# Turning two more head pairs of batch 1 by crossbar DMA, and holding batch 2's loads back, in a fused attention and feed-forward kernel

## The chip, the cores and the metric

The kernel runs on one core of one Trainium2 chip. The metric is device time in microseconds (us) for one execution of the whole program. A profile's span is about 2 us shorter than the time of the same execution.

## The reference, cut to what matters

```python
# q, k, v: (batch 4, heads 8, seq 768, head_dim 64), float32
k_sum = k.reshape(B, H, 24, 32, D).max(axis=3)     # block maxima of the keys
v_sum = v.reshape(B, H, 24, 32, D).mean(axis=3)    # block means of the values
scores = softmax over [ local window of 31 keys | 24 blocks (+ log 32) ]
x = (scores @ [v, v_sum]) as (3072 tokens, 512)
g, val = x @ w_gate, x @ w_val                     # 512 x 1536 each
out = x + sigmoid(x @ w_res) * ((gelu(g) * val) @ w_out)
```

## The kernel before

The 3072 tokens are done in eight units of 384, two for each batch. In unit u TensorE runs twelve feed-forward steps (`fo` 0 to 11), each of four gate and four value products, then the output products of this unit, between which it puts the attention of unit u+1. Scores need keys and queries with head_dim on the partitions, so each pair of heads has to be transposed. For batches 2 and 3 the crossbar does this (DMA transposes issued from SP). For batch 1 TensorE does it in unit 1.

The names in the profiles: `tp` are transposes on TensorE, `g` and `vv` the gate and value products, `gvT` what VectorE makes of both (when it has, their buffers are free for TensorE again), `f` the output products, `s` the scores, `P` their exponentials, which VectorE multiplies by a mask, and `ao` the attention products. `vT` are the transposed values of a batch and `vsT` the block sums that VectorE takes of them. `kW` and `qT` are the transposed keys and queries, `km` and `ks` steps of the rest of the keys (`k_rest`). SPq and POOLq are the queues on which SP and GpSimd issue DMAs.

```python
def load_rows(b):                      # k, q (and v) rows of a batch, by head, issued from GpSimd
    for sb, src, name in (...)[0:2 if b == 1 else 3]:          # k, q, v in this order
        for h in range(H):
            nc.gpsimd.dma_start(out=sb[b][:, h // 2, :, h % 2 * D:...], in_=src[b, h]...)

def load_batch(b):
    load_rows(b)
    for c in range(NC + 1):            # seven value chunks in token order, into vext
        load_values(b, c)

def k_step(b, hp, pool, tag):          # six TensorE transposes, an ACT copy, then the rest
    tp = turn_pair(k_sb[b], hp, pool, tag)
    nc.scalar.copy(kw[:, :, OWN:OWN + QT]..., tp...)
    k_rest(kw)                         # VectorE: block maxima and neighbours, five instructions

def turn_batch(b, p0, p1):             # crossbar: two transposes for k, one for q, per pair
    for hp in range(p0, p1):
        for e in range(2):
            nc.sync.dma_start_transpose(out=kt[:, :, e, OWN:OWN + QT], in_=k_sb[b]...)
        nc.sync.dma_start_transpose(out=qT[b % 2][hp]..., in_=q_sb[b][:, hp]...)

def turn_values(b):                    # crossbar: four transposes, for the block means of v
    ...
# ---- in the loop over units, cut ----
if u == 1: load_batch(2)
for fo in range(FO):
    fo_step(st, gvT, fo)
    values_step(u, fo)     # VectorE: value copies; in units 2 and 4, steps 5 to 8, block_sums(vT)
    if u == 0 and fo == 4: load_batch(1)
    if u == 2 and fo == 8: gate(gvT[0:1, fo, 0:1]); load_rows(3)
    if half == 0 and 1 < nb < B and fo == 0:
        vT[nb] = turn_values(nb); turn_batch(nb, 0, NP - 1)
    if half == 1 and 1 < nb < B and fo == 0: turn_batch(nb, NP - 1, NP)
    if half == 1 and 1 < nb < B and 1 < fo < 2 + NP: k_rest(kW[nb % 2][fo - 2])
    if u == 1 and fo < 8:  # one pair per step: keys in steps 0 to 3, queries in 4 to 7
        ...k_step(nb, hp, *home) or q_step(q_sb[nb], nb, 0, S, hp, *home)
```

`gate` is a tiny GpSimd copy that reads a tile, so that GpSimd issues no later load before this tile is written. A batch's data live in `kW[b % 2]`, `qT[b % 2]` and `vext[b % 2]`.

The softmax here doesn't subtract the row's maximum and nothing guards it: scores larger than these inputs give would overflow.

## Time and profile before

| | |
|---|---|
| time, median of 3 runs | 265.78 us (265.74 to 267.43) |
| span of the profile | 263.4 us |
| TensorE busy | 254.6 us, 97% |
| VectorE, ScalarE busy | 174.0 us, 139.0 us |

GpSimd's timeline (start, length, engine, line, operation, output<-input, count, and in brackets the idle time before and what ended it): it shows when the loads of batch 2 are issued.

```profile
58.76 4.23 POOL L172 DMA_DIRECT2D k_sb<-in_k_dram  x5
64.19 0.83 POOL L172 DMA_DIRECT2D k_sb<-in_k_dram  x1 [1.21 <-DMA vext<-in_v_dram]
65.38 1.64 POOL L172 DMA_DIRECT2D k_sb<-in_k_dram  x2 [0.37 <-DMA vext<-in_v_dram]
67.01 6.75 POOL L172 DMA_DIRECT2D q_sb<-in_q_dram  x8
73.71 6.83 POOL L172 DMA_DIRECT2D v_sb<-in_v_dram  x8
80.48 5.79 POOL L99 DMA_DIRECT2D vext<-in_v_dram  x7
```

The last value chunk is issued at 86.3. The bracketed waits for an earlier DMA fit a program in which each load waits for the one issued eight before it to land. The second view is the tile vT, the transposed values, in the kernel before:

```profile
L233 SPq DMA_TRANSPOSE vT<-v_sb x8: 1213/1229/1288, 89.9 to 152.7; - x8
...
DMA to landing us min/median/max: 2.8/2.8/3.4
```

The four of batch 2 are issued from 89.9 on, 3 us after the last value chunk. They land in a median of 2.8 us (the first in 3.4), and VectorE takes the first block sum without a wait:

```profile
96.22 0.95 DVE L239 TENSOR_REDUCE vsT<-vT 128x24 bf16<-128x768 bf16 x1
```

### The profile page before, as it was taken

What the parts mean: (1) busy time and instruction counts of PE and PEld (TensorE: products, weight loads), DVE (VectorE), ACT (ScalarE), POOL (GpSimd) and SP (SyncE); (2) the same over time, 40 slices, a digit from 0 to 9 for tenths busy, and PEclk for the clock granted to TensorE, in tenths of its full rate; (3) what the DMA queues carried; (4) which work ended last, traced back from release to release, by engine and by line L of the source; (5) the groups of instructions that cost most, each with busy time, mean ns of one, the idle gap of its engine ahead of it and who ended that gap; (6) DMA issues with size and microseconds to landing.
All of it is one profiled execution on the core that took longest, in us unless ns stands there. A gap on an engine that the chain in (4) does not pass through costs nothing.

```text
span 263.4 us, 5865 instructions
## 1 busy us (share of the span) xinstructions
PE 254.6 (97%) x2324; PEld 143.9 (55%) x2324; DVE 174.0 (66%) x414; ACT 139.0 (53%) x240; POOL 93.5 (36%) x124
## 2 busy tenths in 40 slices
PE   6799999999999999999999999999999999999994
PEld 2546555566555555555545565556555665556543
DVE  3744863498476889877837899678738853574424
ACT  2845449657565536754365536653375537553310
POOL 7976533997999107998300000000000000000000
PEclk9999999999999999999999999999999999999999
DMA  5999999999999979999991466224001200020012
GB/s 82 171 172 197 197 206 189 147 177 176 118 117 127 201 126 110 158 173 181 144 48 44 115 119 103 46 82 100 2 1 42 80 0 2 36 86 1 2 40 80
DMA packets 109259, 27.64 MB, mean 105 GB/s; under 512 B 95408, under 2 KB 106288, under 8 KB 109232
## 3 DMA queue, kind: packets, MB, share of 16 engines
q0 software_dynamic: 86032, 16.26, 83.2%
q1 hardware_dynamic: 23200, 11.02, 18.0%
q8 instruction: 18, 0.29, 0.5%
q14 instruction: 9, 0.07, 0.1%
HBM read 32.51 MB, written 6.29 MB: 147 GB/s over the span
## 4 chain that ended last, share of the span: by engine, by line
PE 89%; POOL 3%; DMA 3%; DVE 2%; issue 1%; ACT 1%; POOLq 0%; DVEq 0%
PE f L394 24%; PE g L360 23%; PE vv L360 22%; PE r L378 8%; PE ao L328 4%; DMA vext<-in_v_dram 3%; PE s L296 2%; PE xp L347 2%; POOL vext L99 2%; PE tp L185 1%; PE vs L254 1%; DVE gvT L367 1%; PE gv L360 1%; PE wp L409 1%; POOL k L90 1%
## 5 line engine op out<-in xcount | busy, mean ns | idle before, releaser
L360 PE MATMUL g<-xT,w_gate 128*128 128x384 bf16 x380 | 77.8, 326 | 0.5 <-DVE gvT L367 0.5
L366 ACT ACTIVATE ge<-g 128x384 f32<-128x384 f32 x95 | 46.7, 492 | 59.5 <-PE g L360 30.3
L360 PE MATMUL vv<-xT,w_val 128*128 128x384 bf16 x380 | 77.8, 326 | 0.1
L367 DVE TENSOR_TENSOR gvT<-ge,vv 128x384 bf16<-128x384 f32 x95 | 51.9, 552 | 30.9 <-PE vv L360 27.6
L394 PE MATMUL f<-w_out,gvT 128*128 128x512 bf16 (+2 forms) x312 | 69.5, 363 | 0.0
L360 PEld LDWEIGHTS <-w_val 128*128 128x128 bf16 x384 | 37.5, 98 | 25.6 <-issue 1.0
L360 PEld LDWEIGHTS <-w_gate 128*128 128x128 bf16 x384 | 36.9, 98 | 25.1 <-issue 1.1
L394 PEld LDWEIGHTS <-gvT 128*128 128x128 bf16 x312 | 27.6, 98 | 25.6
L349 ACT COPY xT<-xp 128x384 bf16<-128x384 bf16 x32 | 15.1, 481 | 22.6 <-PE xp L347 22.6
L378 PE MATMUL r<-w_res,xT 128*128 128x512 bf16 x96 | 24.4, 380 | 0.0
L399 DVE SCALAR_TENSOR_TENSOR th<-th,f 128x512 f32<-128x512 f32 (+2 forms) x26 | 16.7, 642 | 11.4 <-PE f L394 8.5
L172 POOL DMA_DIRECT2D k_sb<-in_k_dram x24 | 20.1, 864 | 11.6 <-DMA w_out<-in_moe_w_out_dram 5.2
L99 POOL DMA_DIRECT2D vext<-in_v_dram x28 | 23.2, 866 | 0.9 <-PE g L360 0.6
L384 ACT ACTIVATE th<-r 128x512 f32<-128x512 f32 x24 | 14.2, 602 | 17.4 <-PE r L378 17.4
L313 DVE TENSOR_TENSOR P<-P,maskt 128x768 bf16<-128x768 bf16 x28 | 15.5, 557 | 10.3 <-ACT P L305 7.5
L172 POOL DMA_DIRECT2D q_sb<-in_q_dram x24 | 19.9, 862 | 0.0
L338 DVE TENSOR_TENSOR xn<-ao,rz 128x384 bf16<-128x384 f32 x32 | 17.8, 558 | 1.1
L305 ACT ACTIVATE P<-s,bias_t 128x768 bf16<-128x768 f32 x18 | 16.2, 903 | 3.1 <-PE s L296 2.9
L336 DVE RECIPROCAL rz<-ao 128x6 f32<-128x6 f32 x32 | 6.1, 190 | 17.4 <-PE ao L328 17.4
L401 DVE SCALAR_TENSOR_TENSOR o<-th,xn 128x512 f32<-128x512 f32 (+2 forms) x26 | 16.9, 651 | 0.9
L302 ACT ACTIVATE P<-s,bias_t 128x384 bf16<-128x384 f32 x28 | 14.6, 578 | 0.0
L172 POOL DMA_DIRECT2D v_sb<-in_v_dram x16 | 13.5, 874 | 1.2 <-DMA q_sb<-in_q_dram 0.7
(82 smaller groups left out, 218.4 us busy)
## 6 DMA issues: line engine op xcount, KB each, us to landing
out_dram<-o SPq DMA_DIRECT2D x23, 256.0 KB, 2.6
vext<-in_v_dram POOLq DMA_DIRECT2D x20, 128.0 KB, 6.6
k_sb<-in_k_dram POOLq DMA_DIRECT2D x24, 96.0 KB, 6.1
q_sb<-in_q_dram POOLq DMA_DIRECT2D x24, 96.0 KB, 4.4
w_gate<-in_moe_w_gate_dram POOLq DMA_DIRECT2D x6, 256.0 KB, 8.6
w_val<-in_moe_w_val_dram POOLq DMA_DIRECT2D x6, 256.0 KB, 8.8
w_out<-in_moe_w_out_dram POOLq DMA_DIRECT2D x3, 512.0 KB, 14.1
v_sb<-in_v_dram POOLq DMA_DIRECT2D x16, 96.0 KB, 5.0
```

The costliest lines, as they stand in the source:

```text
L99: nc.gpsimd.dma_start(out=dst, in_=v[b, :, lo:hi, :].rearrange("h p d -> p h d"))
L172: nc.gpsimd.dma_start(out=sb[b][:, h // 2, :, h % 2 * D:h % 2 * D + D], in_=src[b, h].rearrange("(c p) d -> p c d", c=NC))
L305: nc.scalar.activation(P.rearrange("p a t q -> p a (t q)"), s[:, :, 0:TU], AF.Exp, scale=scale, bias=bias_t[:])
L313: nc.vector.tensor_mul(Pf, Pf, maskt.unsqueeze(1).to_broadcast([128, 2 * HT, QT]))
L338: nc.vector.tensor_mul(xn, ao[:, :, :, 0:D], rz.to_broadcast([128, NSUB, 2, D]))
L360: nc.tensor.matmul(acc[:, 0:TU], w[:, ko, fs], st["xT"][:, ko, :], start=(ko == 0), stop=(ko == KO - 1))
L366: nc.scalar.activation(ge[:], g[:, 0:TU], AF.Gelu)
L367: nc.vector.tensor_mul(gvT[:, fo, :], ge[:], vv[:, 0:TU])
L378: nc.tensor.matmul(r[:], st["xT"][:, ko, ss], w_res[:, ko, :], start=(ko == 0), stop=(ko == KO - 1))
L394: nc.tensor.matmul(st["f", sub][:, 0:c1 - c0], gvT[:, fo, ss], w_out[:, fo, c0:c1], start=(fo == 0), stop=(fo == FO - 1))
L399: nc.vector.scalar_tensor_tensor(th, th, 1.0, f[:, 0:c1 - c0], ALU.add, ALU.mult)
L401: nc.vector.scalar_tensor_tensor(o[:, 0:c1 - c0], th, 0.5, st["xn"][:, sub, c0:c1], ALU.mult, ALU.add)
```

## The change

The intent is to free TensorE of half of batch 1's transposes. Pairs 2 and 3 of k and q go to the crossbar at the start of unit 1. Their heads are loaded first. The loads of batch 2 wait for step 6 of unit 1, presumably to leave the DMA engines to the new transposes and batch 1's values. The rests of the two pairs' keys on VectorE follow in steps 10 and 11.

```diff
-                for h in range(H):
+                for h in range(H) if b > 1 else (4, 5, 6, 7, 0, 1, 2, 3):
@@
             if u == 1:
-                load_batch(2)
+                turn_batch(1, 2, NP)
@@
-                if u == 1 and fo < 8:
+                if u == 1 and fo == 6:
+                    gate(gvT[0:1, fo, 0:1])
+                    load_batch(2)
+                if u == 1 and fo in (0, 1, 4, 5):
                     home = TT if fo % 2 else AO
-                    hp, kq = fo % NP, fo // NP
-                    if kq:
-                        q_step(q_sb[nb], nb, 0, S, hp, *home)
+                    if fo < 4:
+                        k_step(nb, fo, *home)
                     else:
-                        k_step(nb, hp, *home)
+                        q_step(q_sb[nb], nb, 0, S, fo - 4, *home)
+                if u == 1 and fo >= FO - 2:
+                    k_rest(kW[1][fo - FO + NP])
```

## The prediction

> **What bounds the kernel now.** I read the page first (busy shares, then the shares of the chain that ended last), then the chain in order of time over unit 1 (53 to 87 us), then the VectorE timeline where that chain could be made to wait, then the DMA view of the stretches into which transfers move.
>
> ```profile
> PE 254.6 (97%) x2324; PEld 143.9 (55%) x2324; DVE 174.0 (66%) x414; ACT 139.0 (53%) x240; POOL 93.5 (36%) x124
> ...
> PE 89%; POOL 3%; DMA 3%; DVE 2%; issue 1%; ACT 1%; POOLq 0%; DVEq 0%
> ```
>
> TensorE is busy 97% of the span and is 89% of the chain. A change that takes TensorE instructions away is worth their place in the stream, as long as no other engine makes TensorE wait for it afterwards. In unit 1 the chain is TensorE without a break:
>
> ```profile
> 57.49 0.34 PE tp L185 x6
> 57.82 0.65 PE g L360 x4
> 58.47 0.65 PE vv L360 x4
> 59.12 0.34 PE tp L185 x6
> ...
> 68.93 1.64 PE vs L254 x7
> 70.57 0.76 PE g L360 x4
> 71.33 0.65 PE vv L360 x4
> ```
>
> One step of the gate and value products is 1.30 us (two pieces of 0.65). A group of six transposes lengthens it by 0.34 us: 56 ns each, not the 219 ns that their row on the page shows, because matmuls are pipelined. This is the first choice I make: 0.34 us and not 6 x 219 ns is the worth of a group.
>
> The second view is VectorE at the end of unit 1, where the change moves work to:
>
> ```profile
> 57.31 0.35 DVE L206 TENSOR_TENSOR km<-kW 128x384 bf16<-128x384 bf16 x1
> ...
> 58.53 0.55 DVE L367 TENSOR_TENSOR gvT<-ge,vv 128x384 bf16<-128x384 f32 x1
> ...
> 72.67 0.79 DVE L269 COPY vext<-vext 32x1536 bf16<-32x1536 bf16 x1
> 73.49 0.55 DVE L367 TENSOR_TENSOR gvT<-ge,vv 128x384 bf16<-128x384 f32 x1
> 74.07 0.96 DVE L274 COPY vext<-vsum 32x768 bf16<-32x768 bf16 x2
> 75.07 0.56 DVE L367 TENSOR_TENSOR gvT<-ge,vv 128x384 bf16<-128x384 f32 x1
> 75.66 0.94 DVE L274 COPY vext<-vsum 32x768 bf16<-32x768 bf16 x2
> 76.70 0.56 DVE L313 TENSOR_TENSOR P<-P,maskt 128x768 bf16<-128x768 bf16 x1
> 77.64 0.56 DVE L313 TENSOR_TENSOR P<-P,maskt 128x768 bf16<-128x768 bf16 x1 [0.39 <-ACT P L302]
> 79.81 0.20 DVE L336 RECIPROCAL rz<-ao 128x6 f32<-128x6 f32 x1 [1.61 <-PE ao L328]
> ```
>
> From 72.67 to 77.26 VectorE runs with hardly a gap. The two mask multiplications (L313) end at 77.26 and 78.20. TensorE's attention products (ao), which need them, start at 79.39 in the TensorE timeline, the second head pair about 0.25 us later. So the masks have 2.1 and 1.45 us of room today. The rest of a pair of keys (L206 to L212) takes 1.22 us from start to the next instruction (57.31 to 58.53).
>
> **What the Trainium skill says.** "TensorE: Matmul & The Clock Gate", Part 4, gives about 275 ns for a 128x128 transpose in a kernel, and its section "Back-to-back issue gap" gives about 81 ns for each product of 128 columns in a stream of weight loads and products, 56 ns isolated. The trace agrees with 56 ns of path. "DMA: Bandwidth & Descriptors", section "Rules for kernel authors", says a transpose next to ordinary DMAs needs nothing, but two transposing streams must not be in flight together. All transposes here come from SP, so there is one stream, as for batches 2 and 3 in the trace (32 transposes). Its section "Issuing engines are not separate DMA queues" says transfers of all issuers run on the same 16 engines and interleave. The trace agrees: a transpose of keys lands in 2.5 us in the median, and in 5.7 us between 104 and 110 us beside loads. "SBUF — State Buffer", section "Who interferes with whom", says certain VectorE copies and GpSimd's descriptor writing block each other. The trace agrees loosely: the spread of values (L266) took 0.70 us at 90.35 with GpSimd idle and 0.99 at 101.17 beside loads, but also 0.70 at 69.63 beside loads.
>
> **The change, part by part.**
>
> Removed from TensorE: four of the eight transpose groups of unit 1 (keys and queries of pairs 2 and 3), 4 x 0.34 = 1.34 us of unbroken chain. Removed from ScalarE: four copies of 0.80 us, which cost the end nothing, since TensorE waits for none of them here.
>
> Added on SP: six DMA transposes, behind unit 0's three output stores. The last store is issued at 56.96, the transposes at about 57.3 to 65 (1.25 us each, as for batch 2). Their sources, loaded first now, have landed by then (queries were issued from 46.56 and took about 4 us). With 6 to 7 us to landing beside loads they are all there by 71 or 72. The key rests come at about 73.7 and the scores of pairs 2 and 3 after 78, so their landing is hidden.
>
> What they delay: the values of batch 1, in flight until about 65.4 (the last 128 KB chunk was issued by 58.2, 7.7 us to landing). Two key and query pairs are 2 x 192 KB in packets of 256 bytes, so 1536 packets. The stretch from 104 to 110 us carried just that many beside loads:
>
> ```profile
> DMA packets 5555, 0.87 MB, mean 146 GB/s; under 512 B 5555, under 2 KB 5555, under 8 KB 5555
> ...
> q0 software_dynamic: 4016, 0.50, 150.1%
> q1 hardware_dynamic: 1539, 0.37, 56.7%
> ```
>
> The software queue moved 4016 packets in 6 us there, against 6332 from 60 to 66 with few others. The difference, 2316 packets at 1055 per us, is 2.2 us. So the values land at about 67.6 instead of 65.4. The block sums (vs L254) now start at 68.77 - 1.34 = 67.4 and wait for each chunk by itself. The last chunk is needed 1.4 us later, at 68.8: about 1 us of room, no wait.
>
> Moved on VectorE: the rests of pairs 2 and 3 go from steps 2 and 3 of unit 1, where VectorE had room, to steps 10 and 11, between the value copies. With TensorE 1.34 us earlier, the product of step 10 starts at 72.2, its copies end at 73.7, the rest of pair 2 at 75.0, the product of step 11 at 75.5, its copies at 76.5, the rest of pair 3 at 77.8, the masks at 78.35 and 78.85. TensorE reaches ao at 79.39 - 1.34 = 78.05. It waits 0.3 us for the first mask and about 0.25 us more for the second: **0.55 us given back**, more if the rests' copies meet GpSimd (one rest took 1.66 us at 58.99). I take 0.6 us. The f products need the last gvT only at their twelfth matmul (about 76.9), so they don't wait.
>
> Moved on GpSimd: the loads of batch 2 start after step 6's product, at about 66 instead of 58.8. 31 issues of about 0.85 us end at 92.5 instead of 86.3. v_sb has landed by about 91; its four transposes start at 88 to 92 and must be there at 95 to 99. Batch 2's first value chunks are needed at 100. Both fit, though their room shrinks to about 1 us. VectorE's value copies at the start of unit 2 now run beside loads: four steps with about 0.3 us more each (0.64 against 0.96 us for the pair of L274). VectorE starts that unit about 1 us late today, and products have buffers for two steps, so this may cost TensorE 0.1 us.
>
> Sum: -1.34 + 0.6 + 0.1 = -0.65 us; 265.78 becomes about 265.2.
>
> **The rivals.**
> 1. The whole 1.34 us arrives (264.4). For it: the chain is TensorE alone in unit 1, and VectorE has 2 us of room before the masks today. Against it: two rests are 2.44 us, more than that room, and just these steps already hold the value copies.
> 2. A transfer becomes the wait. Either the values of batch 1 land after 68.8, or the transposed values or value chunks of batch 2 come after 95 to 100, and TensorE waits 1 to 3 us (266 to 268). For it: transfers fill the DMA engines in both stretches, and landing times of 7 to 8.6 us occur. Against it: sums are awaited by chunk, and held-back loads leave the engines freer after 65 us. I give it one in eight.
> 3. Nothing is seen: the time given back at the masks and at the start of unit 2 eats all (265.8). For it: the slow copies of 0.63 to 0.70 us at 59.85. One in six.
>
> **Range and chances.** The three runs of before span 265.74 to 265.78 with one at 267.43, so the undisturbed spread is small and half a us is readable in paired rounds. Rival 1 sets the low end with some scatter, rival 2's mild form the high end: 264.2 to 266.4, predicted 265.2. Two per cent is 5.3 us, four times the largest gain that the removed groups hold, and more than a late transfer would cost. So within 2% is nearly certain.
>
> **What would show it right or wrong.** Right: in the chain the steps 2, 3, 6 and 7 of unit 1 are 1.30 us without tp. The VectorE timeline has the rests in steps 10 and 11, and the first ao of unit 1 comes 0.6 to 0.9 us earlier than before instead of 1.34, its wait put down to VectorE's P L313. The block sums vs follow the products without a gap. Wrong: ao 1.3 us earlier with no wait (rival 1); a gap before vs named as a DMA of vext, or VectorE waiting for vT in unit 2 until gvT is late for TensorE (rival 2); gaps before g or vv at the start of unit 2 over 0.3 us. If the span differs by more than 1.5 us, the chain must hold a wait that I haven't named.

## The result, and the profile after

The changed kernel took **269.33 us** in the median of 4 runs (268.72 to 269.71), against 266.06 us of before with one more run added. The ratio is 1.011, with a 95% interval from 1.007 to 1.015. Ratios here are the mean time of one kernel's fast runs over that of the other's of the same rounds, so not quite the ratio of the medians. The kernel is about 3 us slower, and the predicted range ended at 266.4.

I cut the span at the first gate product of each unit in TensorE's timeline. The length of a unit is the difference of two such starts. Lengths are steadier than totals, because the start of the program varies between executions: unit 0 of later runs ended at up to 56.0 us instead of 54.4, where the granted clock of the first 30 us was 0.94 instead of 1.00.

| us | to unit 1 | unit 1 | unit 2 | unit 3 | unit 4 | units 5, 6 |
|---|---|---|---|---|---|---|
| before | 54.39 | 33.29 | 29.29 | 29.56 | 29.31 | 28.87, 28.86 |
| after | 54.80 | 32.54 | **32.28** | **30.62** | 29.30 | 28.87, 28.87 |

Unit 1 is 0.75 us shorter, unit 2 is 2.99 us longer, unit 3 is 1.06 us longer. The sum is 3.30 us, the difference of the spans (266.7 and 263.4). Two further differences cancel in it: unit 1 of after starts 0.41 us later, and from the first product of the last unit to the end of the span there are 29.38 us instead of 29.79. The products and VectorE's work of that unit keep their places, so the 0.41 us lie behind them. Why is left open. On the page after, the chain that ended last has changed: TensorE's share fell from 89% to 79%, and a transfer named vT is on it.

```profile
PE 79%; DMA 9%; DVE 7%; issue 3%; ACT 1%; POOL 1%; DVEq 0%; POOLq 0%
```

The chain in order of time (start, length, what) tells where in unit 2:

```profile
88.81 0.65 PE g L360 x4
89.46 0.16 PE vv L360
89.61 8.52 DMA vT<-v_sb
98.14 0.02 issue
98.16 0.04 DVE vsT L239
98.19 0.83 issue
99.03 0.56 DVE gvT L367
99.58 0.04 issue
99.63 0.81 PE vv L360 x4
```

The first transpose of batch 2's values is issued at 89.61 and lands at 98.14, 8.5 us later. VectorE's block sum (vsT) waits for it. Behind the block sum in VectorE's order stands the product gvT that frees the buffer for TensorE's next vv. VectorE's timeline gives the length of its wait:

```profile
98.16 0.95 DVE L239 TENSOR_REDUCE vsT<-vT 128x24 bf16<-128x768 bf16 x1 [2.19 <-DMA vT<-v_sb]
99.03 0.55 DVE L367 TENSOR_TENSOR gvT<-ge,vv 128x384 bf16<-128x384 f32 x1
100.73 0.95 DVE L239 TENSOR_REDUCE vsT<-vT 128x24 bf16<-128x768 bf16 x1 [1.16 <-DMA vT<-v_sb]
```

TensorE's timeline has three waits of vv for gvT in this unit: 1.07, 1.11 and 0.29 us. Counted by the starts of the products, they put TensorE 1.24, 1.27 and 0.45 us back. Up to the first wait, and from the last on, the distances are those of before but for hundredths, so these three are the whole loss of unit 2.

```profile
99.63 0.81 PE L360 MATMUL vv<-xT,w_val 128*128 128x384 bf16 x4 [1.07 <-DVE gvT L367]
```

In unit 3 the same happens with the keys of batch 2's last pair: VectorE waits 1.23 us for kW and TensorE's g 1.54 us for gvT.

Why so late? In after, GpSimd issues batch 2's last loads beside the transposes:

```profile
79.64 6.60 POOL L172 DMA_DIRECT2D v_sb<-in_v_dram  x8
86.14 4.43 POOL L99 DMA_DIRECT2D vext<-in_v_dram  x5
90.76 1.50 POOL L99 DMA_DIRECT2D vext<-in_v_dram  x2 [0.19 <-PE g L360]
```

They end at 92.3 instead of 86.3, as predicted (92.5). The value chunks then need up to 9.6 us to land, so the engines are full from before 89.6 until about 100, just when the four transposes of values run. The DMA view of 89.5 to 99 us has both (the last number is the median of us to landing):

```profile
vext<-in_v_dram POOLq DMA_DIRECT2D x3, 128.0 KB, 9.2
vT<-v_sb SPq DMA_TRANSPOSE x4, 7.9
```

### The profile page after: what moved, and what is told of

It reads as the page before. It is cut to its first block, busy times and chain, and to the rows that moved or that the text cites. A ratio compares the mean times of both kernels' runs of the same rounds, so it can differ in the third digit from the quotient of the medians.

```text
span 266.7 us, 5803 instructions
## 1 busy us (share of the span) xinstructions
PE 253.3 (95%) x2275; PEld 142.9 (54%) x2300; DVE 174.4 (65%) x414; ACT 136.2 (51%) x236; POOL 93.6 (35%) x125
## 3 DMA queue, kind: packets, MB, share of 16 engines
q1 hardware_dynamic: 26464, 11.80, 21.4%
## 4 chain that ended last, share of the span: by engine, by line
PE 79%; DMA 9%; DVE 7%; issue 3%; ACT 1%; POOL 1%; DVEq 0%; POOLq 0%
PE f L394 22%; PE vv L360 19%; PE g L360 18%; PE r L378 7%; PE ao L328 3%; DMA vT<-v_sb 3%; DMA qa<-in_q_dram 3%; DMA kW<-k_sb 3%; PE s L296 3%; DVE gvT L367 2%; PE xp L347 2%; PE vs L254 1%; PE wp L409 1%; DVE vext L274 1%; DVE vsT L239 1%
## 5 line engine op out<-in xcount | busy, mean ns | idle before, releaser
L394 PE MATMUL f<-w_out,gvT 128*128 128x512 bf16 (+2 forms) x298 | 68.6, 362 | 0.7
L378 PE MATMUL r<-w_res,xT 128*128 128x512 bf16 x88 | 23.6, 380 | 0.6 <-issue 0.3
L172 POOL DMA_DIRECT2D k_sb<-in_k_dram x24 | 20.0, 850 | 10.2 <-DMA w_out<-in_moe_w_out_dram 5.2
```

The source lines that it names most:

```text
L172: nc.gpsimd.dma_start(out=sb[b][:, h // 2, :, h % 2 * D:h % 2 * D + D], in_=src[b, h].rearrange("(c p) d -> p c d", c=NC))
L378: nc.tensor.matmul(r[:], st["xT"][:, ko, ss], w_res[:, ko, :], start=(ko == 0), stop=(ko == KO - 1))
L394: nc.tensor.matmul(st["f", sub][:, 0:c1 - c0], gvT[:, fo, ss], w_out[:, fo, c0:c1], start=(fo == 0), stop=(fo == FO - 1))
```

## The experiments

Three causes were open. **Contention**: the late end of batch 2's loads fills the engines when its values are turned. **Rival A**: the six new transposes do the harm. **Rival C**: v rows are loaded too late to be turned. Each run was timed against before in the same rounds; e1 to e4, e5 to e8 and e9 to e11 were on three different chips. The unit lengths are of one profiled execution each.

| | time, median | before, same rounds | ratio (95%) | unit 1 | unit 2 | unit 3 |
|---|---|---|---|---|---|---|
| before (first profile) | | | | 33.29 | 29.29 | 29.56 |
| after (first profile) | 269.33 | 266.06 | 1.011 (1.007 to 1.015) | 32.54 | 32.28 | 30.62 |
| e1 hold only | 270.35 | 266.28 | 1.015 (1.012 to 1.018) | 33.29 | 32.56 | 30.08 |
| e2 no hold | 268.36 | 266.28 | 1.008 (1.006 to 1.010) | 32.24 | 32.48 | 30.54 |
| e3 v rows first | 268.68 | 266.28 | 1.009 (1.007 to 1.012) | 32.54 | 33.46 | 30.55 |
| e4 values turned early | 265.97 | 266.28 | 1.000 (0.998 to 1.003) | 32.79 | 29.30 | 30.42 |
| e5 no value chunks | 265.42 | 266.26 | 0.997 (0.994 to 0.999) | 32.54 | 29.30 | 30.33 |
| e6 e4, rest in step 8 | 265.09 | 266.26 | 0.995 (0.993 to 0.998) | 31.95 | 29.29 | 30.17 |
| e7 e6, last pair in unit 2 | 263.54 | 266.26 | 0.990 (0.988 to 0.992) | 31.95 | 29.29 | 28.96 |
| e8 e7 without the hold | 263.57 | 266.26 | 0.990 (0.988 to 0.992) | 31.94 | 29.30 | 28.87 |
| e9 before, last pair in unit 2 | 265.19 | 265.86 | 0.998 (0.996 to 1.000) | 33.28 | 29.30 | 28.99 |
| e10 e7 again | 263.70 | 265.86 | 0.992 (0.990 to 0.994) | 31.95 | 29.58 | 29.59 |
| e11 e7 with three pairs | 264.40 | 265.86 | 0.995 (0.992 to 0.999) | 31.82 | 29.34 | 28.89 |

All gave correct results except e5.

**e1: the hold alone.**

```diff
 # on before
-            if u == 1:
-                load_batch(2)
+                if u == 1 and fo == 6:
+                    gate(gvT[0:1, fo, 0:1])
+                    load_batch(2)
```

> Before, with nothing changed but the loads of batch 2 held back to step 6 of unit 1 (TensorE still turns all eight groups). Theory (the held loads are still in the queues when batch 2's values are turned, so these transposes land in about 8 us instead of 2.8, and VectorE's block sums make TensorE wait): unit 2 takes about 32.0 us instead of 29.3, unit 3 about 30.3 instead of 29.6, and the whole is 2.5 to 4 us slower than before (268.5 to 270). Rival A (the six new transposes of unit 1 are what disturbs the later units): the hold alone is harmless, 266.0 to 266.5, unit 2 at 29.3.

Unit 2 took 32.56 us, with a median of 8.2 us to landing for batch 2's vT. So the hold by itself, without a single new transpose, brings all of the loss of unit 2. (The total was 270.35, 0.35 us over the range given. Its profile has unit 0 end at 55.9, the slow start; the two runs with a granted clock of 1.00 took 268.92 and 269.65.)

**e2: the new transposes without the hold.**

```diff
 # on after
-                if u == 1 and fo == 6:
-                    gate(gvT[0:1, fo, 0:1])
-                    load_batch(2)
@@
             if u == 1:
+                load_batch(2)
                 turn_batch(1, 2, NP)
```

> The changed kernel with the loads of batch 2 back at the start of unit 1, all else kept (six new transposes, rests of keys in steps 10 and 11, heads 4 to 7 first). Theory: unit 2 is back at 29.3 us and unit 3 at 29.6, unit 1 keeps its 0.75 us (32.5 instead of 33.3), so the whole is 0.3 to 1 us faster than before (265.1 to 265.8). Rival A (the transposes disturb): unit 2 stays at 31 to 32 us and the whole at 268 to 270. Rival B (loads at the start of unit 1 collide with the new transposes and the values of batch 1 come late for the block sums): a wait before vs in unit 1 of 1 us or more, unit 1 over 33.3.

My expectation missed: unit 2 stayed at 32.48. Rival B's wait for the block sums isn't there either: unit 1 took 32.24. By the letter rival A was right, and so was e1 against it. Either half of the change brings the same 3 us, and both together bring no more. GpSimd's timeline of this run shows how:

```profile
63.19 1.65 POOL L172 DMA_DIRECT2D k_sb<-in_k_dram  x2 [1.54 <-DMA vext<-in_v_dram]
65.07 0.82 POOL L172 DMA_DIRECT2D k_sb<-in_k_dram  x1 [0.23 <-DMA vext<-in_v_dram]
68.21 1.64 POOL L172 DMA_DIRECT2D k_sb<-in_k_dram  x2 [2.32 <-DMA vext<-in_v_dram]
...
85.43 6.03 POOL L99 DMA_DIRECT2D vext<-in_v_dram  x7
```

The loads start at 59.1, but GpSimd waits again and again for an earlier load to land, and the last chunk is issued at 91.5 after all. The reason is in the DMA queues. From 57.7 to 72.7 us the software queue, which carries the loads, and the hardware queue, which carries transposes and stores, moved in before and then in e2 (queue, kind: packets, MB, share of 16 engines):

```profile
q0 software_dynamic: 14110, 1.77, 189.8%
q1 hardware_dynamic: 285, 0.52, 10.1%
```

```profile
q0 software_dynamic: 9366, 1.18, 152.5%
q1 hardware_dynamic: 2783, 1.12, 50.6%
```

The loads lost 4744 packets in these 15 us, some 5 us of their pace, while the hardware queue moved 2498 more. So each of these displaced about 1.9 packets of loads (4744 / 2498). (The expectation of e11 says 1.45. That is 4744 / 3264, and it was a slip: the six transposes add 3264 packets over the whole program, 26464 against 23200 on the hardware queue of the two pages, but not all of them had moved by 72.7.) The hold delays the start of batch 2's loads and the transposes delay their progress. The issues end at 92.3 in after, at 91.5 with the transposes alone and at 94.0 with the hold alone (e1, whose unit 1 starts 1.1 us later), and there they meet the transposes of values.

**e3: v rows ahead of k and q rows**, the hold kept.

```diff
 # on after, in load_rows
-for sb, src, name in ((k_sb, ...), (q_sb, ...), (v_sb, ...))[0:2 if b == 1 else 3]:
+for sb, src, name in (rows[2:] + rows[:2] if b == 2 else rows):
```

> The changed kernel, the loads still held to step 6, but batch 2's v rows loaded ahead of its k and q rows; value chunks still last. Theory (contention): the first transpose of values, issued at about 89.6, still shares the engines with the value chunks and lands in 7 to 9 us; the later ones may be issued closer together, so of the 3.0 us lost in unit 2 at least 1 us stays: unit 2 at 30.3 to 32.3, whole 267.5 to 269.3. Rival C (the rows of v arrive too late for their transposes): all of it is gone, vT lands in about 3 us, unit 2 at 29.3, whole 265.5 to 266.3.

Unit 2 took 33.46 us and vT of batch 2 a median of 8.8 us, though its rows had been issued by 73.1. Rival C falls. Unit 2 came out above my range, by 1.2 us: I expected the later transposes to be issued closer together, and they weren't. VectorE's first wait ended only at 99.5. Why this profile lost more than that of after I leave open. It is of the slowest of six runs (269.97 us), and the median, 268.68, is not above that of after, so the larger loss isn't shown to belong to the edit.

**e5: no value chunks of batch 2** (told here since it settles e3's question).

```diff
 # on after, in load_batch; the output is wrong on purpose
-            for c in range(NC + 1):
+            for c in range(0 if b == 2 else NC + 1):
```

> The changed kernel without the seven loads of batch 2's value chunks (its output is wrong on purpose for batch 2: old values stay there). Theory (what slows the transposes of values is the value chunks' packets behind them in the same engines): each vT lands in about 3 us after its issue, no VectorE wait for vT, unit 2 at 29.3, unit 3 at 29.6 to 30.6, whole 264.8 to 266.2. If the packets in flight are not the cause: vT still lands in 8 us and unit 2 stays at 32.

The tile vT in this run:

```profile
L233 SPq DMA_TRANSPOSE vT<-v_sb x8: 1221/1227/1247, 89.7 to 153.2; - x8
...
DMA to landing us min/median/max: 2.8/2.8/2.8
```

With the seven chunks gone, the transposes are issued at the same 89.7 and land in 2.8 us. Unit 2 is back at 29.30. The packets of the value chunks, in flight at the same time, are what cost the 3 us. It is not GpSimd's work of issuing them: in after the last issue ended at 92.3, and the third transpose, issued at 93.95, still took 7.3 us. Unit 3 stays at 30.33, so its loss has another source.

**e4: values loaded first and turned in unit 1.**

```diff
 # on after
 def load_batch(b):
+    if b == 2: v rows, then the value chunks, then k and q rows; return
@@
+                if u == 1 and fo == FO - 1:
+                    vT[2] = turn_values(2)
                 if half == 0 and 1 < nb < B and fo == 0:
-                    vT[nb] = turn_values(nb)
+                    if nb != 2: vT[nb] = turn_values(nb)
```

> The changed kernel, loads held to step 6, with batch 2's v rows and value chunks loaded first, k and q rows after, and the four transposes of values issued in step 11 of unit 1, ahead of the stores. Theory: they may land in 8 us or more, as other loads run, but are there before VectorE's block sums at about 95, so no wait: unit 2 at 29.3, unit 1 at 32.5, whole 265 to 266.2 (unit 3 may keep up to 0.7 us of its 1.1). If late landing were not the cause: unit 2 stays at 31 or more, whole 268 to 270.

Unit 2 is at 29.30. The transposes of batch 2's values are issued from 72.0 now, and some still take up to 10.2 us to land, but they are there long before their sums. Late landing does no harm by itself; it must not be awaited. Two losses are left, both a little larger than I expected: a wait of 0.50 us before ao in unit 1 (32.79 us, 32.5 expected) and one of 1.39 us in unit 3, which keeps 0.86 of its 1.06 us.

**e6: the rest of pair 2 in step 8.**

```diff
 # on e4
-                if u == 1 and fo >= FO - 2:
-                    k_rest(kW[1][fo - FO + NP])
+                if u == 1 and fo in (8, FO - 1):
+                    k_rest(kW[1][2 if fo == 8 else 3])
```

> The version with the values turned early, with the rest of pair 2's keys moved from step 10 to step 8 of unit 1, beside the block sums, where VectorE sits idle for 1.6 us. Theory (two rests between the value copies delay the masks by 2.5 us and cost 0.5 to 0.6 us at ao): the wait of ao for P falls from 0.5 to under 0.1 us, unit 1 from 32.8 to 32.2 or 32.3, whole 0.4 to 0.6 us below the version without it, 265.3 to 265.7. Rival: the 0.6 us come from elsewhere, unit 1 stays at 32.5 to 32.8.

Unit 1 fell to 31.95 us and the wait of ao is gone. That is better than the 32.2 I expected (and 265.09 us in all better than 265.3): the late masks had cost unit 1 of e4 0.84 us, not only the 0.50 of the wait. VectorE's timeline of after shows the masks right behind the second rest, and ao (seen from rz, which follows it) right behind the masks. The first line below is pair 3's last copy:

```profile
78.03 0.21 DVE L212 COPY kW<-ks 128x288 bf16<-128x288 bf16 x1
78.17 1.01 DVE L313 TENSOR_TENSOR P<-P,maskt 128x768 bf16<-128x768 bf16 x2
79.19 0.20 DVE L336 RECIPROCAL rz<-ao 128x6 f32<-128x6 f32 x1
```

In e6 pair 2's rest runs beside the block sums, and the masks come early enough that VectorE itself waits for ao:

```profile
69.25 0.36 DVE L212 TENSOR_TENSOR km<-kW 128x384 bf16<-128x384 bf16 x1
...
77.28 1.01 DVE L319 TENSOR_TENSOR P<-P,maskt 128x768 bf16<-128x768 bf16 x2
78.69 0.20 DVE L342 RECIPROCAL rz<-ao 128x6 f32<-128x6 f32 x1 [0.41 <-PE ao L334]
```

So unit 1 now has all of 33.29 - 31.95 = 1.34 us, the whole worth of the removed transposes.

**e7: the last pair of batch 2 turned in unit 2 too.**

```diff
 # on e6
-                    turn_batch(nb, 0, NP - 1)
+                    turn_batch(nb, 0, NP if nb == 2 else NP - 1)
-                if half == 1 and 1 < nb < B and fo == 0:
+                if half == 1 and 2 < nb < B and fo == 0:
```

> As the previous one, and the key and query transposes of batch 2's last pair are issued in unit 2 with the other three instead of at the start of unit 3. Theory (the wait of 1.4 us in unit 3 is the last pair's keys landing late behind batch 3's loads): the wait of g for gvT in unit 3 is gone, unit 3 falls from 30.4 to 29.0 to 29.3, whole 264.0 to 264.8, 0.5 to 0.8% below before. Rival: the rest of that pair still waits, as batch 3's loads slow the earlier transposes as well, and unit 3 stays at 30 or more.

Unit 3 fell from 30.17 to 28.96 us and TensorE waits for gvT nowhere in it. VectorE in e4 and in e7, at the rest of that pair:

```profile
128.21 0.36 DVE L212 TENSOR_TENSOR km<-kW 128x384 bf16<-128x384 bf16 x1 [1.39 <-DMA kW<-k_sb]
```

```profile
125.87 0.35 DVE L212 TENSOR_TENSOR km<-kW 128x384 bf16<-128x384 bf16 x1
```

The time of 263.54 us was below my range of 264.0 to 264.8.

**e8: e7 without the hold** (the loads at the start of unit 1, as in e2).

> As the previous one, with the loads of batch 2 at the start of unit 1 instead of held to step 6. Theory: with the values turned early and the last pair in unit 2, nothing waits on batch 2 near its landing, so the hold hardly matters: within 0.4 us of the previous one (263.8 to 265). Rival (the hold is what protects unit 1's transposes): a wait for kW or for vext in unit 1, unit 1 over 33, whole 0.8 us or more slower than the previous one.

263.57 against 263.54 us: once nothing is awaited close to its landing, the hold is worth nothing either way.

**e9 and e10: what of this is the change's own.** e9 is before with e7's last edit alone; e10 is e7 once more on the same chip.

> Before, with one edit: the transposes of batch 2's last pair are issued in unit 2 with the other three, as in the version of 263.5 us. Theory (its gain over before is made of 1.34 us of removed TensorE transposes in unit 1 and about 0.6 us from this move in unit 3): unit 1 stays at 33.3, unit 3 falls from 29.6 to 28.9 to 29.0, whole 0.5 to 0.8 us below before (265.4 to 265.8). Rival (the move gains everything, the removed transposes nothing): 263.6 to 264.

> The version with values turned early, rest of pair 2 in step 8 and all pairs of batch 2 turned in unit 2, once more on the same chip as the control without the removed transposes. Theory: 1.2 to 1.6 us below the control, 263.3 to 264.2 us, all of it in unit 1 (31.9 against 33.3).

e9 has unit 3 at 28.99 and unit 1 at 33.28: that edit was worth 0.57 us by units in before as well. Its total is 0.67 us lower (0.2%, its interval just under 1). e10 was 263.70 us, 1.5 us below e9 by the medians, with unit 1 at 31.95 against 33.28. The 1.33 us of unit 1 are the safer measure of the removed transposes: e10 has the other edits too, and 0.4 us of the totals' difference are the shorter stretch at the end of the program (29.78 us in e9's profile from the first product of the last unit, 29.39 in e10's). e10's profile shows small losses in units 2 and 3 (29.58 and 29.59, in unit 3 with a wait of 0.32 us for gvT) that e7's had not, so the later units are not wholly quiet in each execution.

**e11: three pairs by the crossbar.** As e7, with heads 2 to 7 loaded first, the keys of pairs 1 to 3 turned and then their queries, the rests in steps 7, 8 and 11, and two groups left on TensorE.

> As the version of 263.5 us, with pair 1 of batch 1 turned by the crossbar as well (keys of pairs 1 to 3 first, then queries), so nine transposes in unit 1 and two groups left on TensorE. If TensorE alone bounds unit 1: another 0.67 us less, unit 1 at 31.3, whole 262.8 to 263.3. If the longer stream of transposes lands too late (1632 packets more, at the measured 1.45 packets of loads displaced by each about 2.2 us later): TensorE waits for the keys or queries of pair 1 or 3, or block sums for the last value chunk, by 1 us or more, whole 264 or above.

Unit 1 fell by 0.13 us only (31.82) instead of 0.67, and the times scattered from 263.12 to 266.58. The chain shows why in its profile: it leaves TensorE for a transpose of keys and then for VectorE's order.

```profile
59.92 7.98 DMA kW<-k_sb
...
67.99 0.37 DVE km L212
```

```profile
67.99 0.36 DVE L212 TENSOR_TENSOR km<-kW 128x384 bf16<-128x384 bf16 x1 [1.34 <-DMA kW<-k_sb]
```

So it gained next to nothing here. The second expectation comes nearer: VectorE waited 1.34 us for the keys of pair 1, and the median is over 264. But TensorE's timeline has no single wait in unit 1; VectorE's lateness runs on to the masks, and 0.54 of the 0.67 us went there. The profile is of an execution of 263.64 us; what made others take up to 266.58 isn't shown. The version to keep is e7 or e8.

## Why the prediction was wrong

- **Worth of the removed groups, 1.34 us: right.** Unit 1 lost 33.29 - 31.95 = 1.34 us once nothing gave it back (e6).
- **0.6 us given back at the masks: right.** Unit 1 of after was shorter by 0.75 us, so 0.59 came back: ao waited 0.25 us for P and took 0.85 us instead of 0.57. e6 took the cause away and the time came.
- **Packets of the new transposes: mis-sized by half.** I counted k and q of two pairs as 2 x 192 KB, 1536 packets; it is 4 x 192 KB, and the pages show 3264 more. The slope that I had drawn, 1.5 packets of loads per packet (2316 / 1539), was low too (1.9 in e2). That batch 1's values landed nearly where I had them was in part luck: the last at 68.3 us, 67.6 predicted and 65.5 in before, because only some 1900 of the new packets had moved by then. The block sums still didn't wait. In e2 batch 2's loads bore the rest, and their last chunk was issued 5.2 us later (91.5 against 86.3). In after these loads were held back, so this error is not the one that failed.
- **The step that failed: "Both fit, though their room shrinks to about 1 us."** I had worked out where batch 2's loads would end (92.5; measured 92.3) and where its values would be turned (from 88; measured 89.6). I then checked only that the *sources* had landed, and took for granted that a transpose issued at 88 is there at 95. I had the landing times of transposes beside loads before me (5.7 to 8.4 us) and used them for batch 1, but not for vT. With 8.5 us the first vT lands at 98.1, while VectorE was free for it at 96.0. By the 7 to 8.6 us that I name under rival 2, issues at 88 to 92 land at 95 to 100.6, with no room left.
- **Rival 2 was what happened**, in the form that I had named second, and I gave it one in eight. My reason against it, that held-back loads leave the engines freer after 65 us, looked at unit 1 and not at the stretch into which these loads moved. The rival's size, 1 to 3 us, was right for unit 2 (2.99), and unit 3's 1.06 us came on top.
- **Unit 3 was not in the prediction.** Before already lost some 0.6 us there to the last pair's keys (e9), and every profile from after to e6 lost more. e7 shows that issuing this pair earlier removes it. How much of the 1.06 us is later loads of batch 3 and how much a different order of packets isn't settled.
- **Start of unit 2: 0.1 us predicted, none seen.** TensorE's first steps of unit 2 had no wait.

## What to carry to other kernels

When a transfer is moved, look at what will be in flight at its new time and ask which *other* transfer is awaited there: its landing time, not the readiness of its source, is what counts. A transfer that is hidden in 2.8 us with the engines quiet may take 8 us beside loads of short packets, so issue it a stretch earlier rather than clear the engines for it. Put VectorE's moved work where TensorE has a step longer than usual, and cut the span by stage before reading totals: here a gain of 0.75 us and a loss of 4 us stood in different units.

## What the Trainium skill lacked or had wrong

- "DMA: Bandwidth & Descriptors", section "Rules for kernel authors", says a transpose next to ordinary DMAs needs nothing. That held for correctness in every run here that was meant to be correct, but not for time: a transpose of 128x768 bf16 landed in 2.8 us with no loads in flight (e5) and in 8.5 us beside loads (after), and each packet of such transposes displaced about 1.9 load packets (e2). I found no such cost in its section "DMA Transpose (X-bar)".
- "TensorE: Matmul & The Clock Gate", Part 4, gives about 275 ns for a transpose in a kernel, and "Back-to-back issue gap" about 81 ns for products of 128 columns in a stream. Taking 24 transposes out of a busy TensorE made unit 1 1.33 to 1.34 us shorter (e9 against e10, before against e6), which is 56 ns each, the figure that the page gives for the isolated gap.
- "SBUF — State Buffer", section "Who interferes with whom", says that VectorE's copies can be blocked by GpSimd. The trace of before agrees, but shows no steady amount: the first copy of a rest (L210) took 0.20 us all five times that no load was being issued, and 0.20 to 0.70 us the eleven times that one was.
